# Group normalization on one core: loads and stores in runs of three tiles instead of two

## The chip, the cores and the metric

The kernel runs on one core of a Trainium2 chip. The metric is the device time of one execution in microseconds (us). Three runs of the kernel before took 634.19 us in the median (633.79 to 635.87).

The core has five engines, each with its own instruction stream: PE (matrix multiply), DVE (vector), ACT (scalar, with activation functions), POOL (GpSimd) and SP (sync, which only waits and issues DMAs here). Sixteen DMA engines move data between the chip's memory (HBM) and the core's working memory (SBUF, 128 partitions). Engines wait for one another through semaphores.

## The reference

```python
B, G, C, H, W = 128, 32, 1024, 32, 16          # x is bfloat16
xr = x.reshape(B, G, C // G, H, W)
mu = xr.mean(axis=(2, 3, 4), keepdims=True)
var = ((xr - mu) ** 2).mean(axis=(2, 3, 4), keepdims=True)
xn = (xr - mu) / jnp.sqrt(var + 1e-5)
return xn.reshape(B, C, H, W) * g[None, :, None, None] + b[None, :, None, None]
```

Each of the 128 x 32 pairs of sample and group is normalized over its 32 channels x 512 pixels = 16384 values, and then scaled and shifted by a gain and an offset per channel.

## The kernel before

**Tiles.** Four samples with 32 groups each fill the 128 partitions, so one partition holds one sample and group: 16384 bfloat16 values, 32 KiB. A tile is 128 x 16384, 4 MiB. There are NT = 32 tiles. Six buffers `xt0` to `xt5` hold them (NBUF = 6); tile i uses buffer i mod 6, is normalized in place and is stored from there.

**One tile's chain.** Its load lands (semaphore `ld[j]`). PE adds its 32 slices of 512 columns into one PSUM bank by 32 matmuls with an identity matrix (line 148). DVE reduces that to minus the mean (`mean`, line 165). ACT squares the deviations in two halves and sums them (line 278), and forms the standard deviation (lines 292 and 299). DVE takes the reciprocal and makes 32 scales and 32 offsets per partition (lines 179, 182, 189). Then the 32 channels are scaled in place: the first 14 by DVE, the other 18 by POOL (both on line 218, in `scale_on`). When both are done (`s_dve`, `s_pool`), the tile can be stored. Four engines work on neighbouring tiles at once. DVE's `step(i)` begins with the mean of tile i+1 (line 178), before it scales tile i.

**The order of the DMAs.** All big transfers are issued by SP, in program order, and run through one queue. `sync_program` first issues loads 0 to 5. Then it goes through the tiles: it waits until tile i is ready, issues store i (line 123), and after every second tile (`i % RUN == RUN - 1`, RUN = 2) it issues two loads, of the tiles i+5 and i+6 (line 115). A load first waits for the store of the tile that had its buffer (`st[j]`). So the queue's order is loads 0 to 5, stores 0 1, loads 6 7, stores 2 3, loads 8 9, and so on to stores 24 25, loads 30 31, stores 26 to 31. At the end SP waits for all stores (line 129). The other engines' programs don't name RUN.

Of the kernel before, what the change touches and what calls it, by code (L numbers as in the profile page):

```python
# [15 lines left out]
EPS = 1e-5  # L16

NBUF = 6
RUN = 2
MM_FREE = 512  # L20
DVE_SHARE = 14

# [2 lines left out]
def kernel(  # L25
# [15 lines left out]
    NT = B0 // NS  # L41
# [68 lines left out]
    def sync_program(sync):  # L110
        def load(i):
            j = i % NBUF
            if i >= NBUF:
                sync.wait_ge(st[j], 16 * (i // NBUF))
            sync.dma_start(out=xt[j][:], in_=x_v[i]).then_inc(ld[j], 16)

        for i in range(min(NBUF, NT)):
            load(i)
        for i in range(NT):
            j = i % NBUF  # L120
            sync.wait_ge(s_dve, i + 1)
            sync.wait_ge(s_pool, i + 1)
            sync.dma_start(out=o_v[i], in_=xt[j][:]).then_inc(st[j], 16)
            if i % RUN == RUN - 1:
                first = i + 1 + NBUF - RUN
                for n in range(first, min(first + RUN, NT)):
                    load(n)
        for j in range(NBUF):
            sync.wait_ge(st[j], 16 * len(range(j, NT, NBUF)))
# [179 lines left out]
    with tc.tile_critical():  # L309
        with nc.Block() as block:  # L310
            block.sync(sync_program)
            block.tensor(tensor_program)
            block.vector(vector_program)
            block.gpsimd(pool_program)
            block.scalar(scalar_program)
# [30 lines left out]
```

## Time and profile before

| | |
|---|---|
| median of three runs | 634.19 us |
| the profiled execution | 634.93 us |
| its span on the core | 633.2 us |
| HBM read / written | 134.22 MB / 134.22 MB |
| DMA rate over the span | 424 GB/s |
| busy share: PE, DVE, ACT, POOL | 41%, 55%, 75%, 72% |
| time to landing, median: load / store | 19.4 us / 29.3 us |

The page divides the span into 40 slices and gives for each the busy share of the DMA engines and the rate. The timeline lists instructions with their start and length in us; "x2" marks two instructions in one row. SPq rows are DMA issues: the start is when SP issued the transfer, not when it moved data. The time to landing runs from issue until the last of the sixteen DMA engines has reported, so it contains the time that a transfer stands behind others in the queue.

### The profile page before, as it was taken

What the parts mean: (1) busy time and instruction counts of PE and PEld (TensorE: products, weight loads), DVE (VectorE), ACT (ScalarE), POOL (GpSimd) and SP (SyncE); (2) the same over time, 40 slices, a digit from 0 to 9 for tenths busy, and PEclk for the clock granted to TensorE, in tenths of its full rate; (3) what the DMA queues carried; (4) which work ended last, traced back from release to release, by engine and by line L of the source; (5) the groups of instructions that cost most, each with busy time, mean ns of one, the idle gap of its engine ahead of it and who ended that gap; (6) DMA issues with size and microseconds to landing.
All of it is one profiled execution on the core that took longest, in us unless ns stands there. A gap on an engine that the chain in (4) does not pass through costs nothing. (4 is left out here: it accounts for less than half of the span.)

```text
span 633.2 us, 3721 instructions
## 1 busy us (share of the span) xinstructions
PE 259.3 (41%) x1025; PEld 105.8 (17%) x1025; DVE 348.3 (55%) x610; ACT 476.5 (75%) x194; POOL 453.7 (72%) x583
## 2 busy tenths in 40 slices
PE   0977409054180632707327082360823608145000
PEld 0333103021030210302113031120301203012000
DVE  0057777767657175661757617476274762737660
ACT  0499999999959398693976939779397793967900
POOL 0049999999949398593986939769397693977990
PEclk9988858668595685957859577595765957659555
DMA  8999999999999999999999999999999999999986
GB/s 361 429 431 419 431 420 412 435 435 441 431 433 433 431 431 431 426 433 433 433 433 437 433 424 437 428 424 431 431 435 429 428 435 431 439 433 432 436 383 284
DMA packets 9324, 268.57 MB, mean 424 GB/s; under 512 B 1120, under 2 KB 1120, under 8 KB 1120
## 3 DMA queue, kind: packets, MB, share of 16 engines
q1 hardware_dynamic: 9216, 268.44, 98.9%
q8 instruction: 3, 0.05, 0.0%
q14 instruction: 9, 0.07, 0.0%
q10 hardware_dynamic: 96, 0.00, 0.0%
HBM read 134.22 MB, written 134.22 MB: 424 GB/s over the span
## 5 line engine op out<-in xcount | busy, mean ns | idle before, releaser
L218 POOL TENSOR_SCALAR xt<-xt,scl,bia 128x512 bf16<-128x512 bf16 x576 | 452.7, 801 | 163.6 <-DVE xt L218 163.6
L278 ACT ACTIVATE ja<-xt,negmean 128x8192 fp8e5<-128x8192 bf16 x64 | 455.5, 7118 | 123.4 <-DVE jd L165 121.9
L148 PE MATMUL pa<-xt,eye 128*128 128x512 bf16 x1024 | 259.1, 417 | 309.4 <-PEq L146 309.4
L218 DVE TENSOR_SCALAR xt<-xt,scl,bia 128x512 bf16<-128x512 bf16 x448 | 304.2, 753 | 1.2
L148 PEld LDWEIGHTS pa<-xt,eye 128*128 128x128 bf16 x1024 | 105.7, 105 | 462.4 <-issue 368.0
L165 DVE TENSOR_SCALAR_CACHE_REDUCE jd<-pa 128x512 bf16<-128x512 f32 x32 | 21.8, 681 | 165.3 <-PE pa L148 165.3
L179 DVE RECIPROCAL rstd<-std 128x1 f32<-128x1 f32 x32 | 5.2, 162 | 84.9 <-ACT std L299 84.9
L278 ACT ACTIVATION_READ_ACCUMULATOR ja<-xt,negmean 128x1 f32 x64 | 11.9, 186 | 0.0
L182 DVE TENSOR_SCALAR scl<-gb,rstd 128x32 f32<-128x32 f32 x32 | 10.2, 319 | 1.1
L299 ACT ACTIVATE std<-sq,half 128x1 f32<-128x1 f32 x32 | 9.4, 295 | 1.0
L189 DVE SCALAR_TENSOR_TENSOR bia<-scl,negmean,gb 128x32 f32<-128x32 f32 x32 | 8.5, 266 | 1.1
L292 ACT ACTIVATE half<-sq,eps_t 128x1 f32<-128x1 f32 x32 | 8.9, 278 | 0.0
L161 DVE COPY gb<-gb_p 128x64 f32<-128x64 f32 x1 | 0.2, 225 | 10.4 <-PE gb_p L134 10.4
L134 PE MATMUL gb_p<-gb_b,rep 32*128 32x64 bf16 x1 | 0.2, 231 | 11.4 <-DMA gb_b<-in_b_dram 11.4
L273 ACT ACT_TABLE_LOAD x1 | 1.3, 1283 | 1.9 <-issue 1.9
L165 DVE DVE_READ_ACCUMULATOR jd<-pa 128x1 f32 x32 | 2.5, 80 | 0.0
L134 PEld LDWEIGHTS gb_p<-gb_b,rep 32*128 32x128 bf16 x1 | 0.1, 100 | 11.4 <-DMA gb_b<-in_b_dram 11.4
L228 POOL TENSOR_SCALAR_AFFINE_SELECT eye<-ones_b 128x128 bf16<-128x128 bf16 x1 | 0.3, 295 | 0.9 <-DVE ones_b L160 0.9
L160 DVE MEMSET ones_b<- 128x128 bf16 x1 | 0.2, 165 | 1.1 <-SPq L309 1.1
L330 POOL MEMSET const-float32-0.0<- 128x1 f32 x1 | 0.1, 99 | 0.3 <-issue 0.3
L237 POOL TENSOR_SCALAR_AFFINE_SELECT rep<-ones_b 32x128 bf16<-32x128 bf16 x1 | 0.3, 305 | 0.0
L273 ACT ACTIVATE warm<-eps_t 128x1 f32<-128x1 f32 x1 | 0.2, 203 | 0.0
(4 smaller groups left out, 0.5 us busy)
## 6 DMA issues: line engine op xcount, KB each, us to landing
xt<-in_x_dram SPq DMA_DIRECT2D x32, 4096.0 KB, 19.4
out_dram<-xt SPq DMA_DIRECT2D x32, 4096.0 KB, 29.3
gb_b<-in_g_dram ACTq DMA_DIRECT2D x1, 2.0 KB, 6.5
gb_b<-in_b_dram ACTq DMA_DIRECT2D x1, 2.0 KB, 9.9
```

Source lines behind the costliest of these rows:

```text
L134: pe.matmul(out=gb_p[:].rearrange("p a k -> p (a k)"), lhsT=rep[:], rhs=gb_b[:].rearrange("q a k -> q (a k)"), start=True, stop=True,).the ...
L148: m = pe.matmul(out=pa[j][:], lhsT=eye[:], rhs=xt[j][:, k * MM_FREE : (k + 1) * MM_FREE], start=(k == 0), stop=(k == NMM - 1),)
L165: dve.tensor_scalar(out=jd[i % 2][:], in0=pa[i % NBUF][:], scalar1=-inv_n, scalar2=None, op0=ALU.mult, op1=ALU.add, accum_out=col(negmean, i),
L179: dve.reciprocal(out=col(rstd, i), in_=col(std, i))._wait_ge(s_std, c + 1).then_inc(s_dd, 1)
L182: dve.tensor_scalar(out=scl[j][:], in0=gam, scalar1=col(rstd, i), scalar2=None, op0=ALU.mult,)._wait_ge(s_dd, 3 * c + 2).then_inc(s_dd, 1)
L189: dve.scalar_tensor_tensor(out=bia[j][:], in0=scl[j][:], scalar=col(negmean, i), in1=bet, op0=ALU.mult, op1=ALU.add,)._wait_ge(s_dd, 3 * c ...
L218: return eng.tensor_scalar(out=span, in0=span, scalar1=scl[j][:, k : k + 1], scalar2=bia[j][:, k : k + 1], op0=ALU.mult, op1=ALU.add,)
L228: pool.affine_select(out=eye[:], in_=ones_b[:], pattern=[[-1, P]], compare_op=ALU.is_equal, fill=0.0, base=0, channel_multiplier=1,)._wait ...
L273: act.activation(out=warm[:], in_=eps_t[:], func=ACT.Sqrt)
L278: m = act.activation(out=ja[:], in_=xt[j][:, h * F // 2 : (h + 1) * F // 2], func=ACT.Square, bias=col(negmean, i), scale=1.0, accum_out=s ...
L292: act.activation(out=col(half, i), in_=sq[:, 2 * j : 2 * j + 1], func=ACT.Identity, bias=eps_t[:], scale=inv_n,)._wait_ge(s_sq, 3 * c + 1) ...
L299: act.activation(out=col(std, i), in_=sq[:, 2 * j + 1 : 2 * j + 2], func=ACT.Sqrt, bias=col(half, i), scale=inv_n,)._wait_ge(s_sq, 3 * c + ...
```

## The change

RUN becomes 3, and the condition that places the loads is written so that the last loads come right after store 25:

```diff
-RUN = 2
+RUN = 3
@@ sync_program
             sync.dma_start(out=o_v[i], in_=xt[j][:]).then_inc(st[j], 16)
-            if i % RUN == RUN - 1:
-                first = i + 1 + NBUF - RUN
-                for n in range(first, min(first + RUN, NT)):
+            if (NT - NBUF - 1 - i) % RUN == 0:
+                for n in range(max(NBUF, i + 1 + NBUF - RUN), min(i + 1 + NBUF, NT)):
                     load(n)
```

With NT = 32 and NBUF = 6 the condition holds for i = 1, 4, 7, ..., 25 (and for 28 and 31, where no load is left). After store 1 come loads 6 and 7, after store 4 loads 8, 9 and 10, and so on; after store 25 come loads 29, 30 and 31.

## The prediction

> **What bounds the kernel now.** I read the page's DMA rows first, then the sync engine's issues, then the tail engine by engine. "Load n" and "store n" are the DMAs of tile n, 4 MiB each.
>
> ```profile
> DMA  8999999999999999999999999999999999999986
> GB/s 361 429 431 419 431 420 412 435 435 441 431 433 433 431 431 431 426 433 433 433 433 437 433 424 437 428 424 431 431 435 429 428 435 431 439 433 432 436 383 284
> ...
> q1 hardware_dynamic: 9216, 268.44, 98.9%
> ```
>
> One queue carries everything and is busy 98.9% of the span, at about 431 GB/s, in the stretch of loads alone (second slice, 429) as in the mixed slices. ACT (75%) and POOL (72%) have room. Only the last two slices fall, to 383 and 284. So there are two questions: what one transfer takes, and what happens at the end.
>
> ```profile
> start us, us, engine line op out<-in xcount [idle before <-releaser]
> ...
> 269.67 10.01 SPq L115 DMA_DIRECT2D xt<-in_x_dram  x2
> 279.78 0.85 SPq L123 DMA_DIRECT2D out_dram<-xt  x2
> 308.45 9.98 SPq L115 DMA_DIRECT2D xt<-in_x_dram  x2
> 318.53 0.85 SPq L123 DMA_DIRECT2D out_dram<-xt  x2
> 347.38 10.02 SPq L115 DMA_DIRECT2D xt<-in_x_dram  x2
> 357.50 0.85 SPq L123 DMA_DIRECT2D out_dram<-xt  x2
> 386.70 10.00 SPq L115 DMA_DIRECT2D xt<-in_x_dram  x2
> ```
>
> These are the sync engine's DMA issues (start, length, how many). A pair of loads is issued when the pair of stores ahead of it lands, so from one such row to the next lie four transfers and one turn of the queue from loads to stores. Here that is 38.78, 38.93 and 39.32 us; over the twelve cycles from 74.04 to 543.71 it is 469.67 / 12 = 39.14. The shortest are 38.75 to 38.78, so an undisturbed transfer is 9.69 us, and a cycle loses 0.39 us on average (0 to 0.98; the longest is 74.04 to 113.77). In every cycle the next transfer was queued long before, so the loss is inside the queue; I put it to the turn. Now the tail, the timeline of ACT, POOL and sync from three answers:
>
> ```profile
> 553.46 0.34 SPq L115 DMA_DIRECT2D xt<-in_x_dram  x1
> ...
> 573.02 7.12 ACT L278 ACTIVATE ja<-xt,negmean 128x8192 fp8e5<-128x8192 bf16 x1 [8.48 <-DVE jd L165]
> ...
> 587.90 7.11 ACT L278 ACTIVATE ja<-xt,negmean 128x8192 fp8e5<-128x8192 bf16 x1
> ...
> 589.30 14.15 POOL L218 TENSOR_SCALAR xt<-xt,scl,bia 128x512 bf16<-128x512 bf16 x18 [0.98 <-DVE xt L218]
> 604.32 14.14 POOL L218 TENSOR_SCALAR xt<-xt,scl,bia 128x512 bf16<-128x512 bf16 x18 [0.87 <-DVE xt L218]
> ...
> 603.53 15.34 SPq L123 DMA_DIRECT2D out_dram<-xt  x2
> ```
>
> Load 31 is issued at 553.46 and, 19.4 later by its time to landing, lands at 572.9; load 30 (issued 543.71, 19.4) landed at 563.1. Tile 30's chain follows: PE for 8.97, mean, ACT from 573.02 (9.9 after the landing), POOL, store 30 issued at 603.53. Tile 31 is 15.0 behind: store 31 is issued at 618.54 and lands 12.9 later, at 631.4, 1.8 before the span ends at 633.2. Store 30 (18.3 to landing) landed at 621.8. Between load 31 and store 30 the queue does five stores in 48.9, 9.78 each. So store 31 is issued 3.3 before its predecessor lands, and follows it by 9.6, an ordinary transfer. The compute chain of the last pair is just inside the time that the queue needs anyway. That balance is what decides here.
>
> **The change, part by part.** It adds no DMA and takes none away: 32 loads and 32 stores of 4 MiB, all on the sync queue, with the same waits of each. Only their order changes.
>
> (1) Runs of three in the middle. The order becomes stores 2, 3, 4, loads 8, 9, 10, stores 5, 6, 7, loads 11, 12, 13, and so on to stores 23, 24, 25, loads 29, 30, 31, then stores 26 to 31. Queue positions of load 31 (58th transfer) and of the last six stores are as before. Load 31 has 13 turns from loads to stores ahead of it now (after load 5, then after every pair through load 29) and 9 then (after loads 5, 7, 10, 13, 16, 19, 22, 25, 28). At 0.39 each, four fewer save **1.6 us**. Bounds: nine turns at nothing against 13 x 0.39 = 5.1 now, a saving of 5.1; nine at the worst 0.98 are 8.8, a loss of 3.7. I take the mean, since a longer run need not make a turn dearer or cheaper.
>
> (2) Waits moved on the sync engine. Store 4 is issued ahead of load 8 and must be ready first. POOL finishes tile 4 about 15.0 after tile 3, whose store was issued at 99.43: 114.4, and load 8's own wait (store 2 landed) ended at 113.77. That is 0.6 of delay while store 3 still has some 9 us to run in the queue: nothing. Load 8 then lands one transfer later, about 142.8, and ACT, which began tile 8 at 143.3, begins at 152.7; that idles an engine that stands idle some 8.3 to 10.4 us per pair in the middle anyway.
>
> (3) The third store of a run. DVE takes the mean of tile i+1 before it scales tile i (line 178), so a run's last tile waits for the next run's first load. Before, store 29 was issued at 588.39, 25.3 after load 30 landed. Now a run's third store is issued 25.3 after the next run's first load lands, and the queue then still holds two more loads and two stores, 4 x 9.7 = 38.8: 13.5 us of cover. No starvation; without that cover each run would pay the rest.
>
> (4) The tail. The last run is now three loads without a store between. Load 29 lands two transfers before load 31: 572.9 - 19.4 = 553.5, and not 533.8 (issued 514.37, 19.4) as before. ACT begins tile 29 at 553.5 + 9.9 = 563.4; it is free, since tile 28 (its load lands at 514.7) ends near 550. But now ACT has three tiles at 14.9 and POOL three at 15.0 behind the last loads, where before it had two. Store 29 is issued 30.5 after its ACT start (573.02 to 603.53): 593.9; store 30 at 608.9; store 31 at 623.9. The queue is done with store 30 at 621.8, so store 31 finds it **empty**: 623.9 + 12.9 = 636.8, + 1.8 = 638.6, or **+5.4 us**. Bounds from the first tile of a run on PE, which takes 8.36 to 10.02 (rows of the PE timeline) against 8.97: -0.6 to +1.0.
>
> A rule would hide this tail. The Trainium skill ("DMA: Bandwidth & Descriptors", section "Where 436 GB/s comes from") says that for transfers between HBM and SBUF the HBM side, some 358 GB/s, binds. By that a transfer would be 11.7 us as an estimate, five stores 58.6, more than the 51.0 from load 31's landing to store 31's issue, and the change would cost nothing there. The trace has 431 GB/s and 9.69 us, so the cover is 48.9.
>
> Sum: +5.4 - 1.6 = **+3.8 us**. The profiled execution took 634.93 (span 633.2), so its like would take 638.7; the median of the runs is 634.19, 0.74 less, which puts the forecast at **638.0**.
>
> **The rivals.** A measurement can tell about 0.3% (1.9 us) from no change.
>
> A: the turns give the tail back, and the kernel is not slower. Place: the middle; price: up to 5.1. For it: the excess per cycle varies from 0 to 0.98, so it is not a fixed fee, and three queued transfers may let the queue run through a turn. Against: several cycles of pairs already lose nothing. It decides from a saving of 3.5 (nine turns under 0.18 each). With all of it gone: 634.19 + 5.4 - 5.1 = 634.5. To be faster by 0.3% the saving would have to reach 7.3, more than the turns cost, so that needs the tail term to be wrong too.
>
> B: the turns get dearer, since six transfers are mixed in a cycle and engines can drift further apart: +3.7 in place of -1.6, so 634.19 + 5.4 + 3.7 = 643.3. Against: slices with loads alone run no faster than mixed ones.
>
> C: starvation in the middle. If the third store is ready over 13.5 us later than I work out, each of the eight full runs pays the rest; at 1 us each, 638.0 + 8 = 646. Against: ACT idles 8 us and more per pair.
>
> D: that the change does nothing to the order. The changed program's sync order shows the runs of three from store 2 on; only the first pair, loads 6 and 7, stays. I give it no chance.
>
> **How the numbers follow.** Forecast (late last store, part of it paid by fewer turns) 0.67, with its own range from 636.4 (a saving of 2.6 and the warm end of PE) to 640.6 (no saving, cold end). A 0.16, of which 0.04 faster and 0.12 the same. B 0.11, C 0.06. Faster 0.04, same 0.12, slower 0.84. The range reaches down into A, to 635.4, and up toward B, to 641.0.
>
> **What would show it.** Right: store 31 issued 50 to 52 us after load 31 lands, after store 30 has landed, and landing 12.9 later; ACT's last three tiles back to back; load 31 landing at 570 to 573; eight cycles of six transfers at about 58.5 us (6 x 9.69 + 0.39). Wrong: load 31 landing before 569 (A) or after 576 (B); DMA slices in the middle under 400 GB/s (C); or store 31 issued while store 30 is still in the queue, which would take the whole +5.4 away.

## The result, and the profile after

Five runs of the changed kernel took 638.83 us in the median (637.94 to 640.04), five of the kernel before 634.45 (633.79 to 635.87): a ratio of **1.0065, 95% interval 1.0051 to 1.0079**. The change costs 4.4 us. The profiled execution of the changed kernel took 637.94, the shortest of its five, with a span of 636.2.

The page of the changed kernel, its DMA rows:

```profile
DMA  8999999999999999999999999999999999999976
GB/s 360 431 433 409 431 431 402 435 433 433 431 433 437 433 435 433 433 431 435 433 431 431 433 435 424 435 433 431 431 439 433 431 435 433 431 431 438 432 313 264
...
q1 hardware_dynamic: 9216, 268.44, 98.4%
```

The middle is what it was, 424 to 439 GB/s from the eighth slice until the last two. What is lost is lost in those: 313 and 264, where the kernel before had 383 and 284. The sync engine's timeline, DMA issues in the middle (start, length, how many):

```profile
347.36 19.68 SPq L115 DMA_DIRECT2D xt<-in_x_dram  x3
367.15 34.62 SPq L123 DMA_DIRECT2D out_dram<-xt  x3
405.52 19.63 SPq L115 DMA_DIRECT2D xt<-in_x_dram  x3
425.25 34.60 SPq L123 DMA_DIRECT2D out_dram<-xt  x3
463.62 19.80 SPq L115 DMA_DIRECT2D xt<-in_x_dram  x3
```

The runs of three are there, and a cycle of six transfers takes 58.16 and 58.10 us: 9.69 each, so the queue doesn't starve. The stores' issues are drawn out over 34.6 us, since the third waits for the next run's first load, as expected; the queue covers that. Now the tail, timelines of sync, ACT and POOL:

```profile
542.33 0.33 SPq L115 DMA_DIRECT2D xt<-in_x_dram  x1
...
562.59 7.12 ACT L277 ACTIVATE ja<-xt,negmean 128x8192 fp8e5<-128x8192 bf16 x1 [13.57 <-DVE jd L164]
...
577.89 7.12 ACT L277 ACTIVATE ja<-xt,negmean 128x8192 fp8e5<-128x8192 bf16 x1 [0.32 <-ACTq L306]
...
592.77 7.11 ACT L277 ACTIVATE ja<-xt,negmean 128x8192 fp8e5<-128x8192 bf16 x1
...
609.19 14.14 POOL L217 TENSOR_SCALAR xt<-xt,scl,bia 128x512 bf16<-128x512 bf16 x18 [0.87 <-DVE xt L217]
...
608.40 15.35 SPq L123 DMA_DIRECT2D out_dram<-xt  x2
```

Load 31 is issued at 542.33 and lands 29.1 later, at 571.4. ACT works through tiles 29, 30 and 31 with one pause of 0.32 us (562.59, 577.89, 592.77), POOL follows, and stores 30 and 31 are issued at 608.40 and 623.41. Store 30 takes 12.0 to land: 620.4. What the queue does in between is seen in the windows of the same run; the last two columns are the busy share of the DMA engines and GB/s:

```profile
616.00:620.00 4.00, 0.00 (x0) 0.00 (x0) 2.18 (x3) 0.00 (x0) 4.00 (x6) 0.50 0.63 270
620.00:624.00 4.00, 0.00 (x0) 0.00 (x0) 0.00 (x0) 0.00 (x0) 3.34 (x5) 0.50 0.00 0
624.00:628.00 4.00, 0.00 (x0) 0.00 (x0) 0.00 (x0) 0.00 (x0) 0.00 (x0) 0.50 1.13 483
```

In the window from 620 to 624 no packet of a transfer starts, and the one computing engine at work is POOL, on the last tile. Store 31 then has the queue to itself and lands after 11.1, at 634.5.

### The profile page after: what moved, and what is told of

It is laid out like the page before. It is cut to its first block, busy times and chain, and to the rows that moved or that the text cites. A ratio compares the mean times of both kernels' runs of the same rounds, so it can differ in the third digit from the quotient of the medians.

```text
span 636.2 us, 3704 instructions
## 1 busy us (share of the span) xinstructions
PE 256.9 (40%) x1008; PEld 105.6 (17%) x1025; DVE 348.1 (55%) x610; ACT 476.6 (75%) x194; POOL 453.7 (71%) x583
## 6 DMA issues: line engine op xcount, KB each, us to landing
xt<-in_x_dram SPq DMA_DIRECT2D x32, 4096.0 KB, 29.1
```

## Experiments

All of them give the sync engine another order or another length of work; unless said, everything else is the changed kernel or the kernel before. The table has what the traces show. "Turns" counts the changes from loads to stores ahead of load 31; load 31's landing is its issue plus its time to landing; the next two columns count from that landing.

| kernel | last run of loads | turns | load 31 lands | store 31 issued | store 31 lands | median of its runs |
|---|---|---|---|---|---|---|
| before | 2 | 13 | 572.8 | +45.7 | +58.6 | 634.45 |
| changed | 3 | 9 | 571.4 | +52.0 | +63.1 | 638.83 |
| e1 threes, pairs at the end | 2 | 10 | 571.4 | +45.2 | +58.8 | 634.09 |
| e2 pairs, threes at the end | 3 | 12 | 572.6 | +51.6 | +62.7 | 638.09 |
| e3 singles, pairs at the end | 2 | 24 | 572.3 | +46.5 | +58.6 | 634.43 |
| e4 changed, last tile 17/15 | 3 | 9 | 573.1 | +49.8 | +60.9 | 635.47 |
| e5 before, last tile 17/15 | 2 | 13 | 571.5 | +44.4 | +58.6 | 634.27 |
| e6 pairs, four at the end | 4 | 12 | 572.9 | +56.4 | +67.5 | 643.07 |
| e8 fours, pairs at the end | 2 | 8 | 577.2 | +45.5 | +58.1 | 636.92 |
| e9 transfers alone | 2 | 13 | 570.3 | | +58.1 | 633.19 |

### The end or the middle: e1 and e2

```diff
-RUN = 3
+RUNS = [2] + [3] * 6 + [2] * 3      # e1
+RUNS = [2] * 10 + [3] * 2           # e2
@@ sync_program
-            if (NT - NBUF - 1 - i) % RUN == 0:
-                for n in range(max(NBUF, i + 1 + NBUF - RUN), min(i + 1 + NBUF, NT)):
+            if i in ends:            # ends, worked out above: last tile of each run
+                r = RUNS[ends.index(i)]
+                for n in range(i + 1 + NBUF - r, i + 1 + NBUF):
                     load(n)
```

> Runs of three from store 2 to load 25, then three runs of two, so that the order ends as in the kernel before (stores 24 25, loads 30 31, stores 26 to 31). Theory (the loss sits in the tail alone: three tiles are still to be computed behind the last loads): load 31 lands at 571 to 572.8 with ten turns ahead of it; store 31 is issued 45.7 us after that landing, while store 30 is still in the queue, and lands 9.6 after it; 633.0 to 634.4 us, some 4 to 5 below the 638.8 of the changed kernel and not slower than the 634.45 of before. Rival (runs of three themselves cost time in the middle): 18 of 26 middle tiles still go in threes, so 637 to 638.5.

> Runs of two as before up to load 25, and only the last two runs of three (loads 26 to 28, loads 29 to 31). Theory (tail alone): the tail is that of the changed kernel: store 31 is issued 51 to 52 us after load 31 lands, on an empty queue, and lands 11 later, so the end is 62.5 to 63.5 after load 31's landing, where it was 58.6; load 31 lands at 572 to 573; 637.5 to 639.5 us. Rival (the middle costs): two runs of eight, so 634.5 to 635.7.

Beside the kernel before on the same chip, e1 has a ratio of 0.999 (0.998 to 1.0001) and e2 1.0047 (1.0034 to 1.006). Six runs of three in the middle cost nothing; two runs of three at the end cost some 3 us (2.2 to 3.8 by the interval). From e1's trace, the sync engine's last two issues and, from the answer on the second of them alone, its time to landing:

```profile
601.61 15.34 SPq L124 DMA_DIRECT2D out_dram<-xt  x2
...
DMA to landing us min/median/max: 13.6/13.6/13.6
```

Store 31 is issued at 616.6 here, 3.9 before store 30 lands (620.5), so its 13.6 is partly a wait in the queue. It lands 9.6 after store 30, and the hole at the end is gone. Both kernels came out as the theory of the tail has it.

### Shorten the last tile's work: e4 and e5

```diff
+LAST_SHARE = 17
+    def share(i):
+        return LAST_SHARE if i == NT - 1 else DVE_SHARE
-            for k in range(DVE_SHARE):
+            for k in range(share(i)):
-            for k in range(DVE_SHARE, KC):
+            for k in range(share(i), KC):
```

> The changed kernel with tile 31's channels split 17 to DVE and 15 to POOL, where they are split 14 and 18: DVE 17 x 0.68 = 11.6 us, POOL 15 x 0.786 = 11.8, where POOL took 14.15. Nothing else is changed. Theory (the compute chain of the last tile sets the end): store 31 is issued 2.3 earlier after load 31's landing (49.6 and not 52.0), lands 11 later, 636.3 to 636.9 us. Rival (the queue sets the end, and the loss was put into the middle): no change, 638.4 to 639.2.

> The kernel before with tile 31 split 17 to 15, the same edit that took 3.4 us off the changed kernel's median. Theory (with pairs at the end the queue, not the compute chain, sets the end): store 31 is issued 2.3 earlier after load 31's landing (43.4 and not 45.7), but stands behind store 30 for longer and still lands 9.6 to 9.7 after it; 634.0 to 635.2 us, no change from before. Rival (the last tile's compute sets the end in both kernels): 631.9 to 632.6.

The same edit gives two answers. On the changed kernel (e4) the ratio to the kernel before falls to 1.0008 (1.0 to 1.0017), from the 1.0047 that e2, with the same tail, had on the same chip. On the kernel before (e5) it does nothing: 0.9994 (0.9985 to 1.0003). POOL and sync in e4, then sync in e5:

```profile
610.92 11.93 POOL L221 TENSOR_SCALAR xt<-xt,scl,bia 128x512 bf16<-128x512 bf16 x15 [0.87 <-DVE xt L221]
...
610.12 13.13 SPq L127 DMA_DIRECT2D out_dram<-xt  x2
...
603.10 13.13 SPq L127 DMA_DIRECT2D out_dram<-xt  x2
```

POOL's part is 11.93 where it was 14.14, and the two stores are 12.8 apart (610.12 and 622.91) where they were 15.0. The end follows one for one: +60.9, where it was +63.1. In e5 store 31 is issued at 615.9 and takes 14.2, all the time gained going into the queue behind store 30. So in the changed kernel the last tile's compute sets the end, and in the kernel before the queue does. More exactly, its slowest engines do. The trace keeps the time of each of the sixteen reports of a landing (not which engine sent it): store 30's come from 614.9 to 621.8 in the kernel before, so ten of the sixteen had reported when store 31 was issued at 618.5. The median of e4, 635.47, lies below the 636.3 to 636.9 that was expected. It is 2.6 us under that of e2 and 3.4 under that of the changed kernel, while its trace, taken in the slowest of its twelve runs, shows 2.2; where the rest comes from is open.

### One tile more: e6

```diff
-RUN = 3
+RUNS = [2] * 11 + [4]               # sync_program as in e1 and e2
```

> Runs of two as before up to load 27, then one run of four (stores 22 to 25, loads 28 to 31). Theory (every further tile in the last run sets its compute, 14.9 to 15.0 a tile, against 9.7 of transfer): ACT begins tile 28 about 10.2 after its landing, 29.1 before load 31's; store 31 is issued -18.9 + 30.5 + 45.2 = 56.8 after load 31's landing and lands 11.1 later, 67.9, where it was 58.6 in the kernel before and 63.1 in the changed one: 9.3 over before, 643.0 to 644.6 us. Rival (a run's length itself doesn't matter, only that the last run isn't of two): 637.5 to 639.5 as with three.

It took 643.07, a ratio of 1.0133 (1.0119 to 1.0148). ACT and sync in its tail:

```profile
553.74 7.12 ACT L279 ACTIVATE ja<-xt,negmean 128x8192 fp8e5<-128x8192 bf16 x1 [28.49 <-DVE jd L166]
...
568.62 7.11 ACT L279 ACTIVATE ja<-xt,negmean 128x8192 fp8e5<-128x8192 bf16 x1
...
583.90 7.12 ACT L279 ACTIVATE ja<-xt,negmean 128x8192 fp8e5<-128x8192 bf16 x1 [0.32 <-ACTq L308]
...
598.78 7.11 ACT L279 ACTIVATE ja<-xt,negmean 128x8192 fp8e5<-128x8192 bf16 x1
...
614.35 15.29 SPq L124 DMA_DIRECT2D out_dram<-xt  x2
```

Four tiles back to back; the stores are again 15.0 apart. Last runs of two, three and four end 58.6, 63.1 and 67.5 after load 31's landing. A tile more should cost 14.9 to 15.0 of compute less 9.7 of transfer, 5.2 to 5.3. From two to three it is 4.5, since with two the queue, not the compute chain, still sets the end; from three to four it is 4.4, 0.6 of the difference being load 31 itself, which landed 10.3 after load 30 in e6.

### Is there a price per turn: e3, e8, e9, e10

The prediction counted on four turns fewer. e3 has 24 in place of 13, with a transfer always queued at the turn:

```diff
-RUN = 3
+LOADS_AFTER = {1: [6], **{i: [i + 5] for i in range(2, 23)}, 23: [28, 29], 25: [30, 31]}
@@ sync_program, after store i
-            if (NT - NBUF - 1 - i) % RUN == 0:
-                for n in range(max(NBUF, i + 1 + NBUF - RUN), min(i + 1 + NBUF, NT)):
-                    load(n)
+            for n in LOADS_AFTER.get(i, ()):
+                load(n)
```

> One load after each store in the middle (store 2, load 7, store 3, load 8, and so on to store 22, load 27, the load always one store behind, so that a transfer is queued at every turn), then the pairs and the tail of the kernel before. 24 turns from loads to stores ahead of load 31, where there are 13 in the kernel before. Theory (each turn costs 0.39 us on average): load 31 lands 4.3 later, near 577, and the run takes 638 to 640 us. Rival (the lost time is not a price per turn, but comes a few times in a run whatever the order): load 31 lands at 571.5 to 573.5, 633.5 to 635.5 us.

The ratio is 0.9996 (0.9986 to 1.0005), and load 31 lands at 572.3. Eleven turns more cost nothing, so a fixed price per turn, which would have been 4.3 us, is out. Fewer turns are no gain either: with nine, load 31 landed at 571.4 in the changed kernel and at 573.1 in e4, whose order up to there is the same; with thirteen it landed at 572.8 in the kernel before and at 571.5 in e5.

e9 takes the engines' work away:

```diff
-            sync.wait_ge(s_dve, i + 1)
-            sync.wait_ge(s_pool, i + 1)
+            sync.wait_ge(ld[j], 16 * (i // NBUF + 1))
# the loops over tiles of PE, DVE, POOL and ACT are left out
```

> The DMAs of the kernel before in the same order with the same waits on stores, but the whole normalization is left out (means, squares, scales on PE, DVE, ACT and POOL): each store waits for its load alone and writes x back. Theory (the 5 to 6 us that the queue loses up to load 31 over 9.69 a transfer come from the transfers themselves): load 31 lands at 570.5 to 573 and the run takes 632.5 to 635 us. Rival (they come from the engines' own traffic and instruction fetches beside the transfers): load 31 lands near 14.4 + 57 x 9.69 = 566.7, and the run takes 627 to 629.5.

It took 633.19, and load 31 landed at 570.3. That is the theory's side, a little below its range. Counted from load 0's landing, the queue loses 4.5 us here over 57 transfers of 9.69; in the kernels that compute, without e8 and e10, it loses 4.7 to 6.4. So most of that time is in the transfers themselves. It also puts a floor under this order: the whole computation adds 1.6 us to its own transfers (ratio of e9 to the kernel before 0.998, 0.9971 to 0.9989).

e8 goes the other way, to fours in the middle:

```diff
-RUN = 3
+RUNS = [2] + [4] * 5 + [2] * 2      # sync_program as in e1 and e2
```

> Runs of four in the middle (loads 8 to 27), then two runs of two, so that the tail is as before. Theory (the middle is set by the queue as long as it never runs empty): the second store of the new tiles is issued 55.4 after the run's first load lands, with the store ahead of it landing at 58.2, so the queue stays fed by some 1 to 3 us; load 31 lands at 571 to 573.5, 633.5 to 635.5 us. Rival (starvation in the middle, the margin being smaller than the spread of the 16 DMA engines): each of the five runs loses 1 to 4 us, 640 to 652.

It took 636.92, a ratio of 1.0035 (1.0022 to 1.0048): neither side was right. The tail is that of pairs, but load 31 comes at 577.2. PE's timeline shows where, since a tile's matmuls begin when its load has landed and the tile before it is done (start, length):

```profile
233.23 8.74 PE L149 MATMUL pa<-xt,eye 128*128 128x512 bf16 x32 [40.05 <-PEq L147]
242.95 7.07 PE L149 MATMUL pa<-xt,eye 128*128 128x512 bf16 x32 [0.97 <-PEq L147]
252.66 8.75 PE L149 MATMUL pa<-xt,eye 128*128 128x512 bf16 x32 [2.64 <-PEq L147]
263.36 7.07 PE L149 MATMUL pa<-xt,eye 128*128 128x512 bf16 x32 [1.95 <-PEq L147]
```

The starts are 9.72, 9.71 and 10.70 apart: the fourth load, the one before the turn to the stores, lands 1.0 late. By the landings this happens at all seven turns up to the one after load 27, by 0.9 to 1.4 each, and not at the last two, in the pairs. In e8 the last store of a run of four is issued only 13.0 to 14.3 us before it lands (store 9 at 209.10, landing at 222.1), so the queue is nearly dry there. A new theory: the 16 DMA engines drift apart while the queue is full, and then turn one after another at no cost; a queue that runs dry lines them up, and a turn in step costs about 1 us. e10 tests it by draining the queue once a cycle:

```diff
# the kernel before
             if i % RUN == RUN - 1:
                 first = i + 1 + NBUF - RUN
+                if first < NT:
+                    sync.wait_ge(st[j], 16 * (i // NBUF + 1))
```

> The kernel before with one wait more in every cycle: the first of two loads is issued only when both stores ahead of it have landed, so that the queue runs dry once a cycle and the 16 DMA engines begin the two loads together. The time gets longer by the dry stretches themselves, some 1.5 to 2.5 us in each of 13 cycles, 654 to 668 us. What is asked is the second load of a pair, whose landing ends with the turn to the stores. Theory (a turn costs when the engines come to it in step, as in the first two cycles of every run and in the runs of four, and nothing when they have drifted apart): the second load lands 10.4 to 10.9 after the first in nearly every cycle. Rival (a turn's cost has to do with the length of a run or with chance): 9.7 in most cycles and 9.9 to 10.7 in some, as in the kernel before.

It took 678.59 in its one run, above the 654 to 668 that was expected: the dry stretches lose 2.4 to 2.9 us each, where 1.5 to 2.5 had been put down, and the turn behind each costs another 1.07. PE in e10, and then PE in the kernel before:

```profile
223.78 8.62 PE L150 MATMUL pa<-xt,eye 128*128 128x512 bf16 x32 [24.53 <-PEq L148]
234.43 7.07 PE L150 MATMUL pa<-xt,eye 128*128 128x512 bf16 x32 [2.03 <-PEq L148]
266.08 9.65 PE L150 MATMUL pa<-xt,eye 128*128 128x512 bf16 x32 [24.58 <-PEq L148]
276.80 7.07 PE L150 MATMUL pa<-xt,eye 128*128 128x512 bf16 x32 [1.07 <-PEq L148]
```

```profile
289.17 9.48 PE L148 MATMUL pa<-xt,eye 128*128 128x512 bf16 x32 [22.00 <-PEq L146]
298.87 7.07 PE L148 MATMUL pa<-xt,eye 128*128 128x512 bf16 x32 [0.21 <-PEq L146]
327.89 8.90 PE L148 MATMUL pa<-xt,eye 128*128 128x512 bf16 x32 [21.96 <-PEq L146]
337.82 7.07 PE L148 MATMUL pa<-xt,eye 128*128 128x512 bf16 x32 [1.03 <-PEq L146]
```

Second loads of a pair start 10.65 and 10.72 after the first in e10, and 9.70 and 9.93 in the kernel before. Over all thirteen pairs of e10 the landings are 10.5 to 11.0 apart, 1.07 over 9.69 on average and at least 0.85; in the kernel before 7 of 13 pairs lose 0.02 or less. After the dry stretch the first load takes 12.1 to 12.6 rather than 9.69. The price of a turn thus depends on the state of the queue, and not on the length of the run.

The outcome is the one that the theory foretold. Whether the price comes from the drift, the sixteen reports of each landing can tell. The drift is there: in the kernel before, first and last report lie 1.5 us apart at load 0 and 6.4 at load 31; at the second loads of e10 they lie 0.5 to 0.7 apart (1.3 in one pair). In e10 the first report comes as late as the last, 10.5 to 11.0 after that of the load before, so all engines pay together. In the kernel before, in four of the five later pairs that lost 0.2 us or more (from loads 12 and 13 on), the first report was on time, 9.71 to 9.72 after the one before, and only later ones were late. But engines in step are not enough for a dear turn. At the turns after loads 7, 9 and 11 of e9 the reports lie 0.5 to 0.7 us apart, as close as in e10, and these loads land 9.70 to 9.71 after the one before: the turns cost nothing. e9's queue stayed full there, and it leaves the computation out; with it, e4's turn after load 10, reports 1.7 us apart, cost 0.01. So the part of the theory that stands is the dry queue, and that the engines drift apart. That the price comes from engines in step does not stand, and why a queue that has just run dry makes the next turn dear is open.

No order beat the kernel before: e1's 0.999 has an interval up to 1.0001.

## Why the prediction was right

The forecast was 638.0, the median 638.83; +3.8 was worked out, +4.4 measured. Step by step:

- **The middle's waits** (steps 2 and 3): right. Cycles of 58.1 to 59.2 from the second on, no starvation, a run's stores spread over 34.6 to 36.1 us at no cost. Rival C fell.
- **The tail** (step 4): right in its mechanism, shown by e1 (undone: gone), e2 (alone: some 3 of the 4.4 us, the two intervals overlapping), e4 and e5 (the last tile's compute decides in the one and not in the other) and e6 (grows with the run). Store 31's issue was put at 51.0 after load 31's landing and came at 52.0, mostly since ACT began tile 29 10.6 after the landing and not 9.9, which is inside the +1.0 that the prediction allowed for PE.
- **The mis-sized term**: store 31's own 12.9 us. I took it from the kernel before, where that store still stood behind store 30 for 3.3 us. Alone in the queue it takes 11.1 (changed kernel, e2, e4, e6), 1.8 less. With the issue 1.0 later, the tail costs 63.1 - 58.6 = 4.5, and not 5.4.
- **The step that failed**: "at 0.39 each, four fewer save 1.6 us". The losses were real and were in the queue, but dividing them by the number of turns gave a price that doesn't exist: 24 turns cost no more than 13 (e3). The profiled run's load 31 did come 1.4 earlier, which looks like the forecast saving, but the same order came 0.3 later than before in e4, and the order of before came 1.4 earlier in e5. Of the two wrong terms the one is 0.9 too high and the other 1.6 too low, so they partly cancelled: that 638.0 came within 0.8 of the median is in part luck. The tail's 4.5 alone is near the measured 4.4; but e2, with a tail of 4.1 by its trace, cost some 3, so these figures agree to about a us and no better.
- **Rivals** A and B both rested on that price and fell with it.

The rule weighed in the prediction, that the HBM side binds at some 358 GB/s (the Trainium skill, "DMA: Bandwidth & Descriptors", section "Where 436 GB/s comes from"), would have hidden the tail. That section works the figure out as half of a stack's 716 GB/s, which two cores share. With one core at work the queue moved 431 GB/s, and the tail wasn't hidden.

## What to carry to other kernels

When transfers are the bound, the order in the middle matters little as long as the queue never runs dry; look at the end instead, and compare the compute still to be done behind the last load with the transfers still queued. Where a tile's compute is longer than its transfer (here 15.0 and 9.7 us), longer runs of loads pile tiles up there, so keep the last run short. Take the time of a lone transfer from a row where it is alone, and don't turn a scattered loss into a price per event before an experiment has changed the number of events.

## What the runs showed of the hardware that was not expected

- A turn from loads to stores costs 1.07 us on average after the queue has run dry (e10, thirteen pairs), and 0 to 0.9, half of the time under 0.1, in the middle of kernels whose queue stayed full. The first two turns of every kernel that computes cost 0.6 to 1.4.
- A drained queue costs more than the turn: the next load lands 12.1 to 12.6 us after the transfer before it, 2.4 to 2.9 over an ordinary transfer. With the turn that is some 3.7 us a cycle.
- A store of 4 MiB alone in the queue took 11.1 us from issue to landing in four kernels, 1.4 over its 9.69 in a full queue.
- The engines of a queue that stays full fall apart: from the first to the last report of a landing it is 1.5 us at load 0 and 7.0 at store 30 in the kernel before, and 0.7 and 4.6 in e9. Of the 40 later turns that cost 0.2 us or more in the kernels whose queue stayed full, 34 made the last report late and the first not (by under 0.05 us).
